# Decode attention with a streamed K/V cache: the ring of K and V moved to a 2048-byte boundary in every partition

## The chip, the cores and the metric

The kernel runs on one core of a Trainium2 chip. The metric is the device time of one execution in microseconds. The kernel before took 1279.48 us (median of three runs, 1279.21 to 1279.5). A profile of one execution of it is read below; "span" is the time from its first to its last instruction.

## The reference

One token for each of 4 batch rows goes through a pre-norm attention block with a cache of 8192 positions and then through a gated MLP. Everything is bf16.

```python
def _A_ref(x, k_cache, v_cache, wq, wo):          # x: [4, 1, 512]; caches: [4, 32, 8192, 128]
    q = (x @ wq).reshape(B, Sq, 32, 128).transpose(0, 2, 1, 3)
    scores = einsum("bhqd,bhkd->bhqk", q, k_cache) * (128 ** -0.5)
    p = softmax(scores)
    o = einsum("bhqk,bhkd->bhqd", p, v_cache)
    return o.transpose(0, 2, 1, 3).reshape(B, Sq, 4096) @ wo

def _B_ref(x, w_gate, w_up, w_down):              # w_gate, w_up: [512, 1792]; w_down: [1792, 512]
    h = sigmoid(x @ w_gate) * (x @ w_up)
    return h @ w_down

h  = x + _A_ref(layernorm(x), k_cache, v_cache, wq, wo)
h2 = h + _B_ref(layernorm(h), w_gate, w_up, w_down)
```

The two caches hold 2 x 4 x 32 x 8192 x 128 bf16 numbers, 536.9 MB, and every byte of them is read once.

## The kernel before

The work is cut into 32 units (`NU`). A unit is four heads of one batch row. Its K is 8 MiB, and so is its V. One DMA brings the K of a unit into SBUF: each of the 128 partitions receives one contiguous row of 65,536 bytes (a head takes 32 partitions, and each of them 256 positions of 128 numbers). V comes in the same form.

**The ring.** `KV` (line 166) is one SBUF tensor of 3 x 65,536 bytes in each partition. Its slots 0 and 1 take K, by the unit's parity, and slot 2 takes V; only the V of the last unit goes to slot 0. All other weights use the ring too: `wq` lies in slot 2 before the first V, and `wo`, `w_gate`, `w_up` and `w_down` come into slots 1 and 2 when the last K and the last V but one have been used. So do the input `x` and the output. Every DMA of the kernel therefore writes into, or reads from, `KV`.

**The order of transfers.** One queue, SP's, issues all the large loads, in an order written out by hand (lines 531 to 557): `wq`, K of unit 0, K of unit 1, V of unit 0, K of unit 2, V of unit 1 and so on. Before each issue the queue waits until the slot is free: a K waits for the scores of two units before (`t_kd`, line 360), a V for the use of the V before it (`t_vd`, the first matmul of line 414). `wq` is line 531, the K and V loads are line 540, `wo` is line 545, `w_gate` 547, `w_up` 551, and `w_down`, in three pieces, 556. The small load of `x` (line 234) and the store of the result (line 558) are issued on ACT's queue.

**The work of a unit.** `scores` turns K in sixteen chunks of 1024 32-bit words: VectorE transposes a chunk of the ring into one half of `kT` (line 334), and TensorE multiplies it with the unit's queries in `Lq` (line 343, four matmuls a chunk), adding up in one PSUM bank. `maxima` takes the maxima of the scores and lets ScalarE write the exponentials to `E_sb` (lines 361 to 368). `pv` for the unit before multiplies the probabilities in `PTz` with V, straight out of the ring (line 404, 64 matmuls), scales the result into `kT` (line 409) and adds it up over the heads with `lane` (line 414). `weights` transposes `E_sb` into `PTz` (line 374) and sums the row sums with `headw` (line 378). After the last unit come the output projection (line 474), the second layer norm, and the gated MLP (lines 491 to 520); line 528 and 529 write the result into the ring, from where it is stored.

**Where tensors lie.** An SBUF tensor is placed behind the one that was declared before it, from byte 16,512 of each partition on. The first one declared is `KV`, so the ring begins at byte 16,512 (8 x 2048 + 128), and its slots, 65,536 bytes apart, at the same remainder. `kT` follows at byte 213,120, then `Lq` at 221,312, `E_sb` at 222,368, `PTz` at 223,392, `q_all` at 227,488, `mask` at 227,744, `lane` at 227,776, `headw` at 227,968, `part` at 228,480 and the rest.

## Time and profile before

| | before |
|---|---|
| device time, median of 3 runs | 1279.48 us (1279.21 to 1279.5) |
| span of the profiled execution | 1277.7 us |
| device time less span | 1.8 us |
| TensorE busy | 797.8 us (62%) |
| VectorE busy | 763.3 us (60%) |
| ScalarE busy | 58.9 us (5%) |
| share of the 16 DMA engines' time that the packets of SP's queue took | 99.7% |
| bytes read from HBM | 550.77 MB, 431 GB/s over the span |
| granted TensorE clock, mean | 0.822 |

The profiled execution's own device time is not listed apart from its span; what lies outside the span is taken as the 1.8 us between the median of the runs and the span. "Busy" is the time in which an engine executes instructions. The line of the DMA engines and their queue says how full the transfer engines were; the chain of waits, read from its end, says which work the end of the execution hung on.

### The profile page before, as it was taken

How to read it: one execution, taken by the hardware profiler on the slowest of the kernel's cores; microseconds unless marked ns; L12 is line 12 of the kernel's file. 1: busy time of each engine (PE TensorE's matmuls, PEld its weight loads, DVE VectorE, ACT ScalarE, POOL GpSimd, SP SyncE). 2: the span in 40 equal slices, each digit the busy share in tenths (PEclk: the TensorE clock that was granted, in tenths of full speed). 3: DMA queues.
4: the chain of work that ended last, by engine and by line, in shares of the span. 5: the costliest groups of instructions: out<-in, count | busy, mean ns of one | idle time of the engine just before them, and what ended most of it. 6: DMA issues, size and time to landing. Idle time of an engine off the chain costs nothing. (4 is left out here: it accounts for less than half of the span.)

```text
span 1277.7 us, 14121 instructions
## 1 busy us (share of the span) xinstructions
PE 797.8 (62%) x4636; PEld 327.1 (26%) x4636; DVE 763.3 (60%) x917; ACT 58.9 (5%) x114; POOL 5.7 (0%) x22
## 2 busy tenths in 40 slices
PE   1676765557755557655567655567555576555578
PEld 0232222222222223222222222222222232222233
DVE  1876665556665557665567655566655566655571
ACT  2000000000000000000000000000000000000001
POOL 1000000000000000000000000000000000000000
PEclk9988877788877788877788777788777888777888
DMA  9999999999999999999999999999999999999998
GB/s 427 427 425 429 427 455 427 431 427 435 447 427 431 427 437 445 427 431 427 445 437 429 429 427 451 431 429 429 427 453 429 429 429 427 455 427 429 429 429 368
DMA packets 10244, 550.83 MB, mean 431 GB/s; under 512 B 1144, under 2 KB 1152, under 8 KB 1408
## 3 DMA queue, kind: packets, MB, share of 16 engines
q1 hardware_dynamic: 10224, 550.77, 99.7%
q8 instruction: 2, 0.03, 0.0%
q14 instruction: 2, 0.02, 0.0%
q10 hardware_dynamic: 16, 0.01, 0.0%
HBM read 550.77 MB, written 0.00 MB: 431 GB/s over the span
## 5 line engine op out<-in xcount | busy, mean ns | idle before, releaser
L334 DVE STREAM_TRANSPOSE kT<-KV 128x1024 f32<-128x1024 f32 x512 | 615.1, 1233 | 301.1 <-DMA KV<-in_A_k_cache_dram 241.0
L343 PE MATMUL PS<-kT,Lq 128*128 128x512 bf16 x2048 | 586.1, 417 | 320.2 <-DVE kT L334 302.6
L343 PEld LDWEIGHTS PS<-kT,Lq 128*128 x2048 | 209.6, 102 | 697.0 <-issue 623.6
L374 DVE STREAM_TRANSPOSE PTz<-E_sb 32x512 bf16<-32x512 bf16 x128 | 89.9, 703 | 128.9 <-PE PS L414 125.2
L404 PE MATMUL PS<-KV,PTz 128*16 128x512 bf16 x2048 | 116.9, 381 | 0.0
L378 PE MATMUL PS<-part,headw 128*128 128x2 f32 x64 | 18.7, 362 | 100.5 <-DVE PTz L374 100.5
L368 ACT ACTIVATE E_sb<-PS,negm 128x512 bf16<-128x512 f32 x32 | 22.0, 687 | 1141.2 <-DVE negm L366 1141.2
L404 PEld LDWEIGHTS PS<-KV,PTz 128*16 128x16 bf16 x2048 | 58.3, 109 | 56.8 <-issue 13.2
L414 PE MATMUL PS<-lane,kT 128*128 128x4 f32 x256 | 33.6, 255 | 30.9 <-ACT kT L409 30.9
L361 DVE TENSOR_REDUCE part<-PS 128x1 f32<-128x512 f32 x32 | 22.1, 692 | 38.8 <-PE PS L343 38.8
L414 PEld LDWEIGHTS PS<-lane,kT 128*128 128x128 f32 x256 | 31.0, 191 | 46.3 <-issue 44.9
L378 PEld LDWEIGHTS PS<-part,headw 128*128 128x128 f32 x64 | 16.0, 310 | 103.7 <-DVE PTz L374 103.7
L321 PE MATMUL PS<-Lq,headw 128*128 128x512 bf16 x32 | 18.7, 585 | 10.9 <-issue 9.5
L409 ACT ACTIVATE kT<-PS,rsb 128x512 f32<-128x512 f32 x32 | 22.0, 687 | 61.1 <-PE PS L404 61.1
L387 PE MATMUL PS<-Lq 128*128 128x512 bf16 x44 | 13.7, 478 | 0.2 <-issue 0.2
L327 DVE TENSOR_TENSOR Lq<-q_all,mask 128x32 bf16<-128x32 bf16 x32 | 9.7, 303 | 0.0
L453 DVE TENSOR_TENSOR kT<-PS,mask 128x512 bf16<-128x512 f32 x1 | 0.7, 692 | 12.9 <-PE PS L414 12.9
L366 DVE STREAM_TRANSPOSE negm<-mxr 128x32 f32<-128x32 f32 x32 | 6.8, 212 | 1.1
L363 DVE STREAM_TRANSPOSE turn<-part 128x32 f32<-128x32 f32 x32 | 6.8, 212 | 1.1
L387 PEld LDWEIGHTS PS<-Lq 128*128 128x128 bf16 x44 | 4.8, 115 | 8.2 <-issue 5.8
L395 DVE RECIPROCAL rsb<-PS 128x1 f32<-128x1 f32 x32 | 6.5, 202 | 0.7 <-PE PS L378 0.7
L300 PE MATMUL PS<-KV,kT 128*4 128x512 bf16 x32 | 3.6, 627 | 5.1 <-DMA KV<-in_A_wq_dram 5.1
(70 smaller groups left out, 59.5 us busy)
## 6 DMA issues: line engine op xcount, KB each, us to landing
KV<-in_A_wq_dram SPq DMA_DIRECT2D x1, 4096.0 KB, 12.2
KV<-in_A_wo_dram SPq DMA_DIRECT2D x1, 4096.0 KB, 27.5
KV<-in_B_w_gate_dram SPq DMA_DIRECT2D x1, 1792.0 KB, 31.4
KV<-in_B_w_up_dram SPq DMA_DIRECT2D x1, 1792.0 KB, 35.2
KV<-in_B_w_down_dram SPq DMA_DIRECT2D x1, 1024.0 KB, 32.5
KV<-in_A_k_cache_dram SPq DMA_DIRECT2D x32, 49.8
KV<-in_A_v_cache_dram SPq DMA_DIRECT2D x32, 30.8
KV<-in_B_w_down_dram SPq DMA_DIRECT2D x1, 512.0 KB, 33.3
```

Of the source, the lines that this page charges most:

```text
L321: emit("pe", lambda e: e.matmul(bank[bk], headb, zeros, start=True, stop=False, skip_group_check=True), waits, incs=0)
L327: t_lq[u] = emit("dve", lambda e, ix: e.tensor_tensor(dst, bass.AP(raw(q_all), at(ix, 0) * (4 * TU) + 4 * (u - TU * t), [[NU * 4, 128], [1 ...
L334: t_tr[u, c] = emit("dve", lambda e: e.transpose(kT[:, (c % 2) * TW:(c % 2 + 1) * TW], KVw[:, o:o + TW]), w, ch="d2p")
L343: ins = e.matmul(bank[SBK], bass.AP(raw(Lq), ix[-1] * 2 + (128 * t + c % 2), [[528, 128], [1, 128]]), rhs, start=False, stop=False, skip_g ...
L361: a = emit("dve", lambda e: e.tensor_reduce(part[:, 0:1], bank[SBK], AX.X, ALU.max), [t_sc[u, NT - 1], t_pool], ch="d2d")
L368: t_exp[u] = emit("act", lambda e: e.activation(E_sb[:, :], bank[SBK], ACT.Exp, bias=negm[:, 0:1], scale=SCALE, accum_out=part[:, 1:2]), [ ...
L374: return [e.transpose(PTz[32 * q:32 * (q + 1), :].rearrange("p (r q c) -> p r q c", r=4, q=4)[:, :, q, :], E_sb[32 * q:32 * (q + 1), :].re ...
L378: t_sum[u] = emit("pe", lambda e: e.matmul(bank[QB[1]][:, 0:2], headw[:, :], part[:, 0:2], start=True, stop=True), [t_ptz[u], t_selc], ch= ...
L387: emit("pe", lambda e: [e.matmul(bank[XS], Lq[:, 0:128], Lq[:, 0:512], start=True, stop=True) for _ in range(n)][-1], [t_ps0, t_lq[NU - 1] ...
L404: made.append(e.matmul(PS[32 * j:32 * j + 16, ob:ob + 512], lhsT, KV[:, slot * SLOT + 512 * k:slot * SLOT + 512 * (k + 1)], start=(k < 4), ...
L409: t_ocp[u] = emit("act", lambda e: e.activation(O_sb, bank[OBK], ACT.Copy, scale=rsb[:, 0:1]), [t_pv[u], t_rs[u]], ch="a2p")
L414: ins = e.matmul(bass.AP(raw(PS), at(ix, 0) * 4 + (512 * EX + 4 * (u - t)), [[4096, 128], [1, 4]]), O_sb[:, 128 * q:128 * (q + 1)], lane[: ...
```

## The change

The SBUF tensors are declared in another order. `kT`, `PTz`, `Lq`, `headw` and `q_all` now stand in front of the ring, and a tensor `spare` of 96 bytes, that nothing uses, fills the place up to the next multiple of 2048. Nothing else differs: both programs have the same instructions in the same order on every engine, with the same waits; only the addresses of operands in SBUF are others. Since the new declaration adds one line, line numbers from 176 on are higher by one.

```diff
+        kT = SB("kT", [128, 2 * TW], FP32)
+        PTz = SB("PTz", [128, 2048], BF16)
+        Lq = SB("Lq", [128, 528], BF16)
+        headw = SB("headw", [128, 128], FP32)
+        q_all = SB("q_all", [128, NU, 4], BF16)
+        spare = SB("spare", [128, 24], FP32)
         KV = SB("KV", [128, NSL * SLOT], BF16)
-        kT = SB("kT", [128, 2 * TW], FP32)
-        Lq = SB("Lq", [128, 528], BF16)
         E_sb = SB("E_sb", [128, 512], BF16)
-        PTz = SB("PTz", [128, 2048], BF16)
-        q_all = SB("q_all", [128, NU, 4], BF16)
         mask = SB("mask", [128, 8], BF16)
         lane = SB("lane", [128, 32], FP32)
         laneb = SB("laneb", [128, 32], BF16)
-        headw = SB("headw", [128, 128], FP32)
         part = SB("part", [128, 32], FP32)
```

| tensor | first byte before | first byte after |
|---|---|---|
| `KV` (ring) | 16,512 = 8 x 2048 + 128 | 30,720 = 15 x 2048 |
| `kT` | 213,120 | 16,512 |
| `PTz` | 223,392 | 24,704 |
| `Lq` | 221,312 | 28,800 |
| `headw` | 227,968 | 29,856 |
| `q_all` | 227,488 | 30,368 |
| `E_sb` | 222,368 | 227,328 |
| `mask` | 227,744 | 228,352 |
| `lane` | 227,776 | 228,384 |
| `part` | 228,480 | 228,576 |

## The prediction

> **What bounds the kernel now.** I read the strip of the span first, the DMA queues next, then the waits of SP's queue and of VectorE, the groups of instructions, and last the end of the chain.

> ```profile
> PE 797.8 (62%) x4636; PEld 327.1 (26%) x4636; DVE 763.3 (60%) x917; ACT 58.9 (5%) x114; POOL 5.7 (0%) x22
> DMA  9999999999999999999999999999999999999998
> DMA packets 10244, 550.83 MB, mean 431 GB/s; under 512 B 1144, under 2 KB 1152, under 8 KB 1408
> q1 hardware_dynamic: 10224, 550.77, 99.7%
> ```

> No compute engine is busy for more than 62% of the span, while the DMA engines are full in every slice, and the packets of one queue took 99.7% of the time of all 16 engines. So the transfers set the time. The queue issued 71 loads (7 of weights, 32 of K, 32 of V), and 10,224 packets are 144 for each: 128 rows, one for each partition, and 16 more that I read as the completions of the 16 engines (71 x 16 = 1136 of the 1144 packets under 512 B). A row of K or V is therefore one packet of 65,536 bytes, and each engine carries 8 rows of each load.

> Is there time in which the queue has nothing to carry?

> ```profile
> SPq L540 <- PE PS L414: 1124.4, 30, 38.5
> DVE kT L334 <- DMA KV<-in_A_k_cache_dram: 241.0, 31, 14.3
> KV<-in_A_k_cache_dram SPq DMA_DIRECT2D x32, 49.8
> 32.32 2.37 DVE L334 STREAM_TRANSPOSE kT<-KV 128x1024 f32<-128x1024 f32 x2 [14.25 <-DMA KV<-in_A_k_cache_dram]
> 1213.92 2.37 DVE L334 STREAM_TRANSPOSE kT<-KV 128x1024 f32<-128x1024 f32 x2 [7.60 <-DMA KV<-in_A_k_cache_dram]
> 32.32:1213.92 1181.60, 743.07 (x4237) 305.39 (x4237) 731.29 (x867) 44.72 (x92) 0.00 (x0) 0.81 1.00 433
> ```

> The fourth and fifth rows are the moments at which VectorE starts on the first and on the last K, each time released by the DMA. Between the two landings lie 61 loads of 8 MiB, in 1181.60 us: 19.370 us for a load. The sixth row, of the view by windows, gives that stretch a full DMA share and 433 GB/s. SP waits 1124.4 us for free slots, which looks like a stall and is none: a K lands 49.8 us after its issue, the V issued just before it and it take 2 x 19.37 = 38.7 us, so about 11.1 us of older work still stands in the engines when the slot comes free. The engines never run dry. On the other side VectorE waits 241.0 us in 31 units for K, 7.8 us a unit. Compute has that much to spare in each unit.

> ```profile
> 1241.51 33.33 DMA KV<-in_B_w_down_dram
> 1274.88 0.60 PE PS L520 x8
> 1275.51 0.43 PE PS L520 x4
> 1275.96 0.41 DVE KV L528
> ```

> The end of the chain agrees: it waits for the last piece of `w_down`, and then 1274.84 to 1277.7 is all that is left, 2.9 us. The time is the pace of the transfers times their number, with small ends.

> **The change, part by part.** It adds, removes and moves no instruction, no DMA and no wait, and no queue is passed. What it alters is addresses: (a) where each row is written, (b) where engines read the ring, (c) where the small tensors lie.

> (a) This alone touches the bound. There are 71 loads with 8 rows an engine, 568 rows one after the other on each engine. All began 128 bytes past a multiple of 256; all begin on one now. Their lengths (65,536, 32,768, 14,336, 8192, 4096 and 2048 bytes) are multiples of 256, so before, a row touched one 256-byte block more than its length needs: the first half used, the last half used. The trace has no row that begins aligned, so the cost of this is bounded from both sides. One engine's share of the pace is 8 x 65,536 bytes in 19,370 ns, 27.07 bytes in a nanosecond; 128 bytes are 4.73 ns. If an engine writes only the bytes that it has and a part block costs it no slot, the gain is 0. If the unused half at the row's start takes its time but the last block ends where the data ends, it is 4.73 ns a row, 568 x 4.73 = 2.69 us. If both part blocks are paid as whole ones, it is 9.46 ns a row, 5.37 us. A loss in (a) by itself I exclude: the aligned row holds no more blocks than the shifted one. I take the middle value, 2.69 us. It is 0.20% of a row of 2421 ns (19,370 / 8), and a cost of that size can stand in the pace without showing anywhere in these rows; that is also why I cannot exclude 0.

> [...]

> [...]

> What is late next, if rows get shorter? Nothing new. A load that lands 0.04 us earlier takes that from VectorE's 7.8 us of waiting, and from the 11.1 us of older work nothing is taken but the same 0.04 us at each load.

> (b) and (c), the engines.

> ```profile
> L334 DVE STREAM_TRANSPOSE kT<-KV 128x1024 f32<-128x1024 f32 x512 | 615.1, 1233 | 301.1 <-DMA KV<-in_A_k_cache_dram 241.0 <-PE PS L343 46.6
> L374 DVE STREAM_TRANSPOSE PTz<-E_sb 32x512 bf16<-32x512 bf16 x128 | 89.9, 703 | 128.9 <-PE PS L414 125.2 <-ACT E_sb L368 0.7
> L404 PE MATMUL PS<-KV,PTz 128*16 128x512 bf16 x2048 | 116.9, 381 | 0.0
> L414 PE MATMUL PS<-lane,kT 128*128 128x4 f32 x256 | 33.6, 255 | 30.9 <-ACT kT L409 30.9
> ```

> In (b) the transposes read chunks of 4096 bytes and the V matmuls 1024 bytes, from starts that move from 128 past a multiple of 256 to a multiple of it. In (c) `kT` and `Lq` keep their remainder to 256 (128); the others shift by multiples of 32 bytes. No row shows these instructions at another address. They hide in the 7.8 us a unit, and that cover holds far: the sixteen transposes of a unit would have to go from 1.233 us to 1.72 us each (7.8 / 16 = 0.49 more), or the four of line 374 with their 2.8 us a unit nearly to four times their length, before K is waited for no longer. So (b) and (c) are 0 in the loop. On the path at the end only the matmuls of line 520 and the copy of line 528 stand, 0.60 + 0.43 + 0.41 = 1.44 us; a tenth of it either way is 0.14 us, which I drop.

> Sum: 2.69 us off the span, 1277.7 to 1275.0. With the 1.8 us outside, and against the median of the runs, 1279.48 - 2.69 = **1276.8 us**, 0.21% less.

> **The rivals.**

> *The writes do not care.* An engine writes 128 bytes in half the time of 256, so the two part blocks together take what one whole block takes, and a row costs the same wherever it begins. For it: nothing in the trace points to a cost that comes with each row rather than with each byte. Against it: the engines have no unused time in which such a cost could hide, and the smallest ones would not show in these rows. Time: 1279.5 us.

> *Both part blocks are paid whole.* As worked out above, 5.37 us: 1274.1 us. Against it: a row's end would then be paid beyond its last byte, which asks more of the engine than the other two cases do. [...]

> *The neighbours of the ring collide.* `kT`, which VectorE writes and TensorE reads through nearly all of a unit, lay right behind slot 2; it lies now close in front of slot 0, the slot of the even units' K. If a partition's memory serves neighbouring addresses one at a time, writes of the 16 even K loads would wait for it. The price, from a stretch of the profile in which the transfers did run slower:

> ```profile
> 1164.00:1241.00 77.00, 48.45 (x281) 20.02 (x281) 46.87 (x56) 2.93 (x6) 0.00 (x0) 0.82 0.98 425
> ```

> 425 against 433 GB/s is 1.9%, 0.36 us a load, and 16 of those are 5.8 us: 1285.3 us. The queue has no idle time, so each nanosecond counts; the rival decides from 0.16 us for each of the 16 loads on (2.56 us in all). Against it: the same neighbourhood stood at slot 2 before, through 31 loads of V, and the pace over K and V together was 433 GB/s; and a window cuts packets at its ends, 16 x 65,536 bytes or 3% of what 77 us carry at 425 GB/s, so that the 425 may be no slower pace at all. For it: the trace cannot show what a load without a neighbour costs.

> That the change might not do what it says is no rival here: the ring's first byte is settled at build time, 30,720.

> **How the numbers follow.** A measurement of this kernel can tell a change of about 0.2%, 2.56 us, from none. The forecast lies just beyond that, so its chance splits. The forecast (half a block a row) has 0.38, of which 0.22 come out faster by over 0.2% and 0.16 within it. Writes that do not care have 0.28, all within. Both blocks have 0.10, all faster. Colliding neighbours have 0.20, all slower. The 0.04 that is left is for small shifts of (b) and (c) at the ends, within. Together: faster 0.32, same 0.48, slower 0.20. The range goes from both blocks, 1274.1, to the far end of the collision, 1285.3; the forecast with the two cases beside it lies within 1274.1 to 1279.5.

> **What would show it.** The stretch from the first K's landing to the last one's (61 loads) is the test: 1181.60 us now; 61 x 8 x 4.73 ns less, 1179.3, by the forecast; unchanged if the writes do not care; 1177.0 with both blocks; 1184 or more if neighbours collide, and then even units' K would land later than odd ones'. The means of 1233 ns (transposes) and 381 ns (V matmuls) should stay within 1%, VectorE's wait for K near 240 us, and the end after the last `w_down` at 2.9 us. The forecast is wrong if the stretch keeps its length, or if the time goes while the stretch stays, which would put the cause at the ends.

## The result, and the profile after

The changed kernel takes 1276.89 us (median of 21 runs, 1276.54 to 1277.38), the kernel before 1279.17 us (21 runs, 1278.81 to 1279.5): 2.28 us less. The ratio is 0.9983, with a 95% interval of 0.9976 to 0.9989. The two sets of runs do not overlap.

The page of the changed kernel, the lines that answer to those of before (line numbers are higher by one):

```profile
span 1275.6 us, 14073 instructions
PE 779.7 (61%) x4588; PEld 328.5 (26%) x4636; DVE 762.3 (60%) x917; ACT 59.0 (5%) x114; POOL 5.7 (0%) x22
DMA packets 10244, 550.83 MB, mean 432 GB/s; under 512 B 1144, under 2 KB 1152, under 8 KB 1408
q1 hardware_dynamic: 10224, 550.77, 99.7%
L335 DVE STREAM_TRANSPOSE kT<-KV 128x1024 f32<-128x1024 f32 x512 | 614.4, 1232 | 300.3 <-DMA KV<-in_A_k_cache_dram 237.5
L405 PE MATMUL PS<-KV,PTz 128*16 128x512 bf16 x2048 | 117.0, 381 | 0.0
KV<-in_A_k_cache_dram SPq DMA_DIRECT2D x32, 49.6
```

The same packets, the same bytes, the engines as full as before: only the bytes move a little faster, 432 GB/s in place of 431. The transposes (1232 ns, 1233 before) and the V matmuls (381, 381) did not notice that the ring moved, and VectorE still waits 237.5 us for K (241.0 before). The 48 TensorE matmuls fewer are taken to be records missing from the trace: the weight loads, 4636, are as many as before.

The 1.8 us that were put between the span and the device time before the change came from a profile and a median of different executions. Where both are known of one execution, 1.2 to 1.3 us lie outside the span, before and after. The profiled execution before the change was thus about 0.5 us faster than the median of 1279.48 us that the forecast started from.

Where the 2.1 us of span went is read from three moments: the first and the last landing of a K, in the timeline of VectorE, and the last landing of all, in the chain.

```profile
32.27 2.37 DVE L335 STREAM_TRANSPOSE kT<-KV 128x1024 f32<-128x1024 f32 x2 [14.21 <-DMA KV<-in_A_k_cache_dram]
1212.12 2.37 DVE L335 STREAM_TRANSPOSE kT<-KV 128x1024 f32<-128x1024 f32 x2 [7.42 <-DMA KV<-in_A_k_cache_dram]
```

```profile
1239.80 32.91 DMA KV<-in_B_w_down_dram
1272.75 0.60 PE PS L521 x8
1273.39 0.43 PE PS L521 x4
1273.85 0.41 DVE KV L529
```

| stretch | before, us | after, us | difference |
|---|---|---|---|
| start to first K | 32.32 | 32.27 | -0.05 |
| first K to last K, 61 loads | 1181.60 | 1179.85 | -1.75 |
| last K to last piece of `w_down`, 8 loads | 60.92 | 60.59 | -0.33 |
| from there to the end | 2.9 | 2.9 | 0.0 |

The gain comes with the loads, and none of it is in the work after the last landing. In the 61 loads it is 1750 ns over 61 x 8 = 488 rows of an engine, 3.6 ns a row of 2421; by the device time it is 2.28 us over 568 rows, 4.0 ns.

The 3.6 ns is too little, because the first loads blur it. The K of unit 2 is the next one that VectorE waits for, three loads after the first; its rows in the timeline, before and after:

```profile
91.53 2.37 DVE L334 STREAM_TRANSPOSE kT<-KV 128x1024 f32<-128x1024 f32 x2 [0.86 <-DMA KV<-in_A_k_cache_dram]
91.74 2.37 DVE L335 STREAM_TRANSPOSE kT<-KV 128x1024 f32<-128x1024 f32 x2 [1.21 <-DMA KV<-in_A_k_cache_dram]
```

The first three loads took 59.21 us before and 59.47 after. The other 58, from the K of unit 2 to the last K, took 1122.39 us before and 1120.38 after: 2.01 us over 58 x 8 = 464 rows, 4.33 ns a row, from 2418.9 ns to 2414.6. These 58 loads are called the steady stretch below.

### The profile page after: what moved, and what is told of

It reads as the page before. It is cut to its first block, busy times and chain, and to the rows that moved or that the text cites. A ratio compares the mean times of both kernels' runs of the same rounds, so it can differ in the third digit from the quotient of the medians.

```text
span 1275.6 us, 14073 instructions
## 1 busy us (share of the span) xinstructions
PE 779.7 (61%) x4588; PEld 328.5 (26%) x4636; DVE 762.3 (60%) x917; ACT 59.0 (5%) x114; POOL 5.7 (0%) x22
## 2 busy tenths in 40 slices
DMA  9999999999999999999999999999999999999998
DMA packets 10244, 550.83 MB, mean 432 GB/s; under 512 B 1144, under 2 KB 1152, under 8 KB 1408
## 3 DMA queue, kind: packets, MB, share of 16 engines
q1 hardware_dynamic: 10224, 550.77, 99.7%
HBM read 550.77 MB, written 0.00 MB: 432 GB/s over the span
## 4 chain that ended last, share of the span: by engine, by line
DMA 60%; PE 20%; DVE 12%; issue 2%; ACT 1%; SPq 0%; DVEq 0%
DMA KV<-in_A_k_cache_dram 58%; PE PS L344 14%; DVE kT L335 12%; PE PS L405 5%; DMA KV<-in_B_w_down_dram 3%; ACT kT L410 1%; PE PS L415 0%; SPq L541 0%; DVE PTz L375 0%; PE PS L521 0%; DVE KV L529 0%; SPq L557 0%; DVEq L112 0%
## 5 line engine op out<-in xcount | busy, mean ns | idle before, releaser
L335 DVE STREAM_TRANSPOSE kT<-KV 128x1024 f32<-128x1024 f32 x512 | 614.4, 1232 | 300.3 <-DMA KV<-in_A_k_cache_dram 237.5
L375 DVE STREAM_TRANSPOSE PTz<-E_sb 32x512 bf16<-32x512 bf16 x128 | 89.9, 703 | 129.1 <-PE PS L415 125.5
L405 PEld LDWEIGHTS PS<-KV,PTz 128*16 128x16 bf16 x2048 | 58.9, 111 | 56.3 <-issue 13.6
L415 PE MATMUL PS<-lane,kT 128*128 128x4 f32 x256 | 33.6, 255 | 31.0 <-ACT kT L410 31.0
L362 DVE TENSOR_REDUCE part<-PS 128x1 f32<-128x512 f32 x32 | 22.1, 691 | 38.7 <-PE PS L344 38.7
L388 PE MATMUL PS<-Lq 128*128 128x512 bf16 x27 | 11.0, 462 | 2.9 <-issue 2.5
L322 PEld LDWEIGHTS PS<-Lq,headw 128*128 128x128 bf16 x32 | 3.5, 108 | 12.8 <-issue 11.3
```

The costliest lines, as they stand in the source:

```text
L335: t_tr[u, c] = emit("dve", lambda e: e.transpose(kT[:, (c % 2) * TW:(c % 2 + 1) * TW], KVw[:, o:o + TW]), w, ch="d2p")
L362: a = emit("dve", lambda e: e.tensor_reduce(part[:, 0:1], bank[SBK], AX.X, ALU.max), [t_sc[u, NT - 1], t_pool], ch="d2d")
L375: return [e.transpose(PTz[32 * q:32 * (q + 1), :].rearrange("p (r q c) -> p r q c", r=4, q=4)[:, :, q, :], E_sb[32 * q:32 * (q + 1), :].re ...
L388: emit("pe", lambda e: [e.matmul(bank[XS], Lq[:, 0:128], Lq[:, 0:512], start=True, stop=True) for _ in range(n)][-1], [t_ps0, t_lq[NU - 1] ...
L405: made.append(e.matmul(PS[32 * j:32 * j + 16, ob:ob + 512], lhsT, KV[:, slot * SLOT + 512 * k:slot * SLOT + 512 * (k + 1)], start=(k < 4), ...
L415: ins = e.matmul(bass.AP(raw(PS), at(ix, 0) * 4 + (512 * EX + 4 * (u - t)), [[4096, 128], [1, 4]]), O_sb[:, 128 * q:128 * (q + 1)], lane[: ...
```

## Experiments: the ring's start, or the neighbours?

Theory A: a row whose first byte lies inside a 256-byte block costs more. Theory B: it was the tensors that moved away from slot 2. Theory C: the start must be a multiple of 2048. Two kernels separate them. Both were run 11 times, next to 21 runs of the kernel before with a median of 1279.20 us.

**e1_front128** keeps the old order and shifts everything by 128 bytes:

```diff
+        front = SB("front", [128, 32], FP32)
         KV = SB("KV", [128, NSL * SLOT], BF16)
         kT = SB("kT", [128, 2 * TW], FP32)
```

> The order of tensors of the kernel before is kept; only a tensor of 128 bytes stands in front of the ring, which then begins at byte 16,640 = 65 x 256 (256 past a multiple of 2048). kT and all others stay behind the ring, 128 bytes further on. Theory A (a row whose first byte lies inside a 256-byte block costs more): the gain of the change comes back whole, about 1276.9 us. Theory B (what moved away from slot 2 gave the gain): no gain, 1279.2 us. Theory C (the start has to be a multiple of 2048): no gain, 1279.2 us.

Measured: 1276.84 us, ratio 0.9983 (0.9974 to 0.9992).

**e2_ring128** keeps the new order and puts the ring back to 128 past:

```diff
-        spare = SB("spare", [128, 24], FP32)
+        spare = SB("spare", [128, 56], FP32)
         KV = SB("KV", [128, NSL * SLOT], BF16)
```

> The changed order of tensors is kept, with kT, PTz, Lq, headw and q_all in front; the filler is 128 bytes longer, so the ring begins at 30,848, 128 past a multiple of 2048. Theory A: the gain is gone, 1279.2 us. Theory B: the gain stays, 1276.9 us. Theory C: gone, 1279.2 us.

Measured: 1278.94 us, ratio 0.9999 (0.999 to 1.0008).

The stretch from the first K to the last, in the view by windows (length first, granted clock, DMA share and GB/s last), of the changed kernel, of e1_front128 and of e2_ring128:

```profile
32.27:1212.12 1179.85, 727.36 (x4206) 306.62 (x4237) 730.33 (x867) 44.77 (x92) 0.00 (x0) 0.81 1.00 434
```

```profile
32.32:1212.02 1179.70, 725.40 (x4206) 305.53 (x4237) 730.80 (x868) 44.72 (x92) 0.00 (x0) 0.81 1.00 434
```

```profile
32.21:1214.01 1181.80, 728.25 (x4206) 306.01 (x4237) 730.54 (x868) 44.76 (x92) 0.00 (x0) 0.81 1.00 433
```

e1_front128 has the whole gain with every tensor in its old place behind the ring, at a start that is 256 past a multiple of 2048. e2_ring128 has none of it with every tensor in its new place. B and C fall, A stands: with the ring at 128 past a multiple of 256 the time was 1279.20 us (before) and 1278.94 us (e2_ring128), with it at a multiple of 256 1276.89 us (after) and 1276.84 us (e1_front128). The steady stretch shows it too: 2415.0 ns a row in e1_front128 (2414.6 after), 2418.9 in e2_ring128 (2418.9 before). The three loads ahead of it took 59.14 us and 59.44 us: they vary by 0.3 us between executions, and not with the ring's start.

## Experiments: is the price paid for each row?

2 us are too few to study a price. If it is paid for each row, sixteen times as many rows make it sixteen times as large. So the rows of K and V are cut into 16 pieces of 4096 bytes; so that no piece continues the one before it, a load becomes two DMAs, one to the even places and one to the odd ones. By the count of before, 128 rows and 16 packets more for each DMA, SP's queue then has an estimated 134,128 packets: 1040 for each of these 128 DMAs and 144 for each of the seven weights'. K and V are permuted alike, so the sums stay what they were.

```diff
-        toks = {x: prog.token(x[0] + str(slots[x]), 16) for x in order}
+        toks = {x: prog.token(x[0] + str(slots[x]), 32) for x in order}
...
-            prog.dma("sp", f"{x}{slot}", lambda e, src=src, slot=slot: e.dma_start(reg(slot, 0, SLOT), src), [w],
-                     tok=toks[x, u])
+            prog.dma("sp", f"{x}{slot}", lambda e, src=src, slot=slot: [e.dma_start(
+                reg(slot, 0, SLOT).rearrange("p (a b f) -> p a b f", b=2, f=2048)[:, :, i],
+                src[:, SLOT // 2 * i:SLOT // 2 * (i + 1)].rearrange("p (a f) -> p a f", f=2048)) for i in range(2)], [w],
+                     tok=toks[x, u], n=2)
```

> The changed kernel, with each row of K and V of 65,536 bytes written as 16 pieces of 4096 bytes: two DMAs a load, the first half of a row to the even places and the second half to the odd ones, the same for K and V. Each engine then writes 64 x 8 x 16 = 8192 pieces and 56 rows of weights. The ring begins at a multiple of 2048. By itself it gives the base for the next run: no less than 1277 us, and more by 8192 - 512 = 7680 times whatever any row costs wherever it begins.

> The same with the ring at 30,848, so that every piece begins 128 past a multiple of 256. The change's 2.28 us over 568 rows were 4.0 ns a row. Theory A: 8248 rows x 4.0 ns, 33 us over the run with aligned pieces (39 us at 4.73 ns a row). Theories by which the cost goes with bytes, or with what lies beside the ring: 2.3 us or nothing.

Measured, in one run each: 1314.37 us aligned, 1351.31 us at 128 past. The windows from the first K to the last, r4k_0 and then r4k_128, and what SP's queue waited for in r4k_128 (us in total, times, longest):

```profile
32.97:1247.21 1214.24, 728.48 (x4206) 306.71 (x4237) 730.94 (x867) 44.72 (x92) 0.00 (x0) 0.81 1.02 422
```

```profile
33.60:1284.25 1250.65, 741.51 (x4206) 309.57 (x4237) 727.56 (x868) 44.72 (x92) 0.00 (x0) 0.80 1.03 410
```

```profile
SPq L541 <- PE PS L415: 427.1, 30, 23.2
```

The difference is 36.94 us (33 to 39 were expected), and in the windows 36.41 us over 61 x 128 = 7808 rows: 4.66 ns a row. The price is paid for each row. Compute did not set this: the DMA share is full in both windows (1.02 and 1.03), and SP, which is held longer by each K's DMA of 1024 rows (median 9.7 us in r4k_0, 0.4 with rows of 64 KiB), still stands idle 427.1 us in r4k_128 for want of a free slot. The base, r4k_0, tells something too: 37.5 us over the changed kernel for 7680 rows more, 4.9 ns for a row that begins aligned. So part of a row's price, 4.9 ns here, is there without a start off the boundary.

## Experiments: what in the row's place is paid for?

The prediction had taken the unused bytes ahead of the row's start to be what is paid for. At 128 past they are as many as those behind the row's end, so other starts have to tell. Of r4k_128 only the filler changes: `[128, 40]` puts the ring at 64 past, `[128, 72]` at 192 past.

> As r4k_0, with the ring 64 bytes past a multiple of 2048, so every one of 8248 rows of an engine begins 64 bytes inside a 256-byte block and ends with a part block of 64 bytes. r4k_128 lay 36.9 us over r4k_0, 4.5 ns a row. If the unused bytes ahead of the row's start cost their time (head rule): half of that, 18.5 us over r4k_0, about 1332.9 us. If the unused bytes behind its end do (tail rule): 192 of 128, 55.4 us, about 1369.8 us. If one more block costs a fixed price: 36.9 us, about 1351.3 us.

> The same with the ring 192 bytes past a multiple of 2048. Head rule: 55.4 us over r4k_0, about 1369.8 us. Tail rule: 18.5 us, about 1332.9 us. Fixed price: 36.9 us, about 1351.3 us.

Measured: 1351.32 us and 1351.39 us, the same as 1351.31 at 128. The windows, r4k_64 and then r4k_192:

```profile
33.46:1284.15 1250.69, 755.75 (x4237) 307.15 (x4237) 728.03 (x868) 44.74 (x92) 0.00 (x0) 0.80 1.02 410
```

```profile
33.55:1284.19 1250.64, 731.52 (x4237) 303.04 (x4237) 729.47 (x867) 44.74 (x92) 0.00 (x0) 0.80 1.03 410
```

Neither the head rule nor the tail rule holds; the price is the same at all three starts (1250.64 to 1250.69 us in the windows, 1214.24 us in that of r4k_0). Then the source was moved instead, for all units but the last (these two kernels compute with other numbers than the reference):

```diff
+            src = bass.AP(src.tensor, src.offset + (64 if u < NU - 1 else 0), src.ap)
```

> As r4k_0, ring at a multiple of 2048, but the loads of K and V of all units but the last read from 128 bytes later in HBM, so that the numbers read are not the reference's; sizes and order stay. If the cost hangs on where the written row begins: 0 over r4k_0, 1314.4 us. If it hangs on the read side as well: 62 of 64 loads pay, about 36 us, 1350 us. If it hangs on the difference of the two sides: 36 us too, 1350 us.

> Source shifted by 128 bytes as in r4k_s128_d0, and the ring at 128 past a multiple of 2048 as in r4k_128. If the written side alone counts: as r4k_128, 1351.3 us. If both sides count and add up: about 1387 us; if the longer of both counts: 1351.3 us. If the difference of the two sides counts: back near r4k_0, about 1315.5 us (the last unit's loads and the weights still differ).

Measured: 1313.34 us with the ring aligned and 1351.19 us with the ring at 128 past, against 1314.37 and 1351.31 without the shift. The windows from the first K to the last, r4k_s128_d0 and then r4k_s128_d128:

```profile
32.97:1247.28 1214.31, 746.96 (x4237) 306.67 (x4237) 730.55 (x867) 44.73 (x92) 0.00 (x0) 0.80 1.02 422
33.47:1284.01 1250.54, 751.66 (x4237) 307.52 (x4237) 728.11 (x868) 44.72 (x92) 0.00 (x0) 0.79 1.03 410
```

They are those of r4k_0 and r4k_128 within 0.11 us; the 1.03 us in the time of the first stand behind the last K. A read that begins 128 bytes later shows no price, and it neither adds to the price of the write nor cancels it. In these kernels the price of the start, 36.2 to 36.4 us in the windows, came with the written side alone. That does not show that such a read costs the engine nothing: if reading has time to spare, a longer read would not be seen.

Last, is it the start off the boundary, the part blocks at both ends, or the one block more? Pieces of 3968 bytes (15.5 blocks) can be laid so that these differ. From the fourth load on, these kernels leave out the last 128 bytes of every piece.

```diff
-                reg(slot, 0, SLOT).rearrange("p (a b f) -> p a b f", b=2, f=2048)[:, :, i],
+                reg(slot, 0, SLOT).rearrange("p (a b f) -> p a b f", b=2, f=2048)[:, :, i, 0:w4],
...                                               # w4 = 2048 for the first three loads, then 1984; the source is cut the same way
```

> As r4k_0, with the ring at a multiple of 2048, but from the fourth load of K and V on each piece leaves out its last 128 bytes: 7808 pieces of an engine are 3968 bytes long, begin at a multiple of 256 and end half way in a block (the 128 bytes left out keep what an earlier load put there, so the output is not the reference's). They touch 16 blocks, as the 4096 bytes did. If a part block at the end is paid as a whole one: as r4k_0, 1314.4 us. If it costs its bytes alone: 7808 x 4.73 ns = 36.9 us less, 1277.5 us. If each part block adds a fixed price: 1277.5 + 35 = 1312.5 us.

> The same with the ring 128 past a multiple of 2048: the 7808 pieces begin half way in a block and end at a block's end, and touch 16 blocks too. If the price is for a start off the boundary: 35 us more than g_0 (and 2 us for the 440 other rows). If it is for a block more than the length needs, the two-part-block case only: only those 2 us more than g_0.

Measured: 1280.86 us and 1282.52 us. g_128 begins every piece off the boundary and pays nothing for it beyond the 2 us expected for its other rows (1.7 measured). g_0 came out 3.4 us over the 1277.5 that the bytes alone would give.

> As g_0 and g_128 (7808 pieces of 3968 bytes, the last 128 of each piece left out), with the ring 64 bytes past a multiple of 2048. A piece begins 64 bytes inside a block and ends 64 bytes before a block's end: two part blocks, but 16 blocks in all, as few as its length allows. If the price is for a block more than the length needs: as g_128, about 1282.5 us. If it is for having a part block at both ends: 7808 x 4.5 ns = 35 us more, about 1317.5 us.

> The same with the ring 192 bytes past a multiple of 2048. A piece begins 192 bytes inside a block and ends 64 bytes inside another: two part blocks, and 17 blocks, one more than its length needs. Both rules say 35 us more than g_128, about 1317.5 us. If the long part block of 192 bytes was what cost time in g_64, it is absent here and the time stays near 1282.5 us.

Measured: 1278.69 us and 1351.12 us. g_64 is 4 us below the 1282.5 expected for "a block more", and 39 us below the other value; part blocks at both ends cost nothing in it. g_192 was a miss for every theory: 68.6 us over g_128 where 35 were expected, and the same 1351 us as r4k_64, r4k_128 and r4k_192, though it carries 3% fewer bytes. The windows, g_0, g_128, g_64 and g_192:

```profile
32.90:1216.00 1183.10, 726.98 (x4206) 306.40 (x4237) 731.33 (x867) 44.75 (x92) 0.00 (x0) 0.81 1.02 420
```

```profile
33.58:1217.68 1184.10, 725.82 (x4206) 305.13 (x4237) 730.05 (x868) 44.76 (x92) 0.00 (x0) 0.81 1.02 419
```

```profile
33.65:1213.83 1180.18, 746.01 (x4237) 306.25 (x4237) 730.47 (x867) 44.75 (x92) 0.00 (x0) 0.81 1.02 421
```

```profile
33.54:1283.87 1250.33, 755.79 (x4237) 307.95 (x4237) 727.58 (x868) 44.75 (x92) 0.00 (x0) 0.79 1.03 397
```

That miss tells the cases apart. Take the steady stretch of each kernel, from the landing of the K of unit 2 to that of the last K in the timeline of VectorE, and divide it by its rows: 58 x 128 = 7424 in the cut kernels. In the g kernels all of these have 3968 bytes.

| kernel | bytes of a row | starts past 256 | blocks touched | ns a row | ns a block |
|---|---|---|---|---|---|
| r4k_64 | 4096 | 64 | 17 | 160.00 | 9.41 |
| r4k_128 | 4096 | 128 | 17 | 160.00 | 9.41 |
| r4k_192 | 4096 | 192 | 17 | 160.00 | 9.41 |
| g_192 | 3968 | 192 | 17 | 160.00 | 9.41 |
| g_64 | 3968 | 64 | 16 | 150.66 | 9.42 |
| g_0 | 3968 | 0 | 16 | 151.23 | 9.45 |
| g_128 | 3968 | 128 | 16 | 151.23 | 9.45 |
| r4k_0 | 4096 | 0 | 16, all full | 155.38 | 9.71 |

In the four runs with 17 blocks a written row took 9.41 ns for each 256-byte block that it touches (160.00 / 17), whether 4096 bytes of them are used or 3968. The windows printed above, over all 61 loads and their 7808 rows, agree: 160.18, 160.18, 160.17 and 160.13 ns a row in r4k_64, r4k_128, r4k_192 and g_192, against 155.51 in r4k_0. The kernel before fits the same line without being used for it: 257 x 9.412 = 2418.9 ns, and 2418.9 were measured in its steady stretch.

r4k_0 lies off that line, by half a block. My estimate for it is a second limit, fitted to r4k_0: the row's bytes at the same pace, 32 half blocks of 4.706 ns, 150.6, and 4.8 ns on top, 155.4. In the fit, the row takes the longer of the two; no run shows the limit itself. For 3968 bytes it is 145.9 + 4.8 = 150.7 ns, and sixteen blocks are 150.6, so g_0, g_64 and g_128 should be alike; they are within 0.6 ns, and why g_0 and g_128 lie 0.6 above the fit is not shown. The changed kernel checks the fit: 512 x 4.706 + 4.8 = 2414.3 ns, and 2414.6 were measured. The fit gives 4.6 ns a row for the change, and its steady stretch 4.33.

## Why the prediction was right, and where it was not

It forecast 1276.8 us, and 1276.89 were measured. That it came so near is luck. The forecast was taken from 1279.48 us, the median of three runs, and 21 runs give 1279.17: it began 0.31 us too high and took off 0.41 us too much (2.69 for 2.28). Point by point:

- *The transfers set the time, and the engines never run dry.* Right. The gain is a pace in the steady stretch (38.69 to 38.72 us from one K to the next before, 38.59 to 38.67 after), the end after the last `w_down` is 2.9 us as before, and VectorE's wait for K stayed, 241.0 to 237.5 us.
- *Edits (b) and (c) are worth 0.* Right. For (c), e2_ring128 has all the new places and no change in time. For (b), which moves with the ring in every run, it rests on the profile: the means of lines 335 and 405 stayed within 1 ns, and VectorE still waits for K. The rival of colliding neighbours, 1285.3 us, falls by e2_ring128 too. Its sign, even units' K later than odd ones', did not show either: from unit 7 on it is the odd units' K that come 0.06 us late (38.67 us after the K before, and the even ones 38.61), and they do so in e1_front128 too, with the old neighbours. Why is not shown.
- *A price for each of 568 rows.* Right, and shown by the kernels with sixteen times the rows: 36.41 us over 7808 rows.
- *4.73 ns a row, 2.69 us.* About right in size: 4.66 ns in the windows of the cut rows, 4.33 ns in the steady stretch of this change, and 2.28 us in the device time, 15% less than forecast. The stretch from the first K to the last was to be 1179.3 us and is 1179.85. Of the 0.55 us between them, 0.37 lie in the first three loads, which vary by 0.3 us between runs, and 0.19 in the row's 4.33 ns for 4.73.
- *The unused half at the row's start takes its time, the last block ends where the data ends.* Wrong, and this is the mechanism that the forecast chose. The middle one of its three values, 4.73 ns a row, was the author's estimate; no run shows a price for the unused half. At 64 and at 192 past, the price should have been half and one and a half times that at 128; it is the same (1351.32, 1351.31 and 1351.39 us at 64, 128 and 192). And g_128, with half a block unused at the start of each row, takes the same 151.23 ns as g_0 with none. On the read side there was no such price either: 1214.31 us from the first K to the last with the source moved by 128 bytes, 1214.24 without.
- *Both part blocks are paid whole, 9.46 ns a row, 1274.1 us.* This rival named the right event, a whole block more (9.41 ns measured), and the wrong sum. It overlooked that an aligned row does not run at the pace of its blocks alone: in r4k_0 it took 155.38 ns, where 16 blocks at 9.412 ns are 150.6. By the fit, an estimate, an aligned row is held 4.8 ns above its bytes, so that of the 9.41 ns of the 257th block 4.8 were paid anyway. So the forecast met the number with the middle of its three values, and for another reason than it gave. That 9.41 less 4.8 comes near half a block is put down to chance: the 4.8 ns come from rows that begin and end on a boundary.
- *Writes that do not care, 1279.5 us.* Wrong for this kernel's rows. But g_64 and g_128 show a shifted start without any loss, where the row touches no block more: 150.66 and 151.23 ns a row, 151.23 in g_0.
- *The bound of 0.2%.* The chances split on whether the gain would pass 2.56 us. It is 0.17% (0.11 to 0.24), just inside; 21 runs of each kernel tell it from none.

## What to carry to other kernels

When the profile shows the DMA engines full from end to end, look at what each row costs beyond its bytes. In these kernels it paid to lay the destination in SBUF so that its rows touch as few 256-byte blocks as their length allows, by starting at a multiple of 256, for which 128 bytes of filler were enough (e1_front128, 1276.84 us for 1279.20). The worth was one number a row, so multiply it first: for rows that fill their blocks it was about half a block, 4.3 to 4.6 ns, 0.2% of a row of 64 KiB and 3% of one of 4 KiB. For rows that leave half a block empty, a bad start cost a whole block, 9.3 ns (g_192 against g_64, 1250.33 and 1180.18 us in the windows), 6%; these needed no start at a multiple of 256 (g_64, g_128), only one at which they touch no block more. And to find out a price that moves the time by 2 us, build a kernel in which it is paid sixteen times as often.
